# The start of a sorted-attention and maxout kernel on TensorE: queries loaded by head pair, the value turn inside the sinkhorn's waits, shared block-diagonal steps, weights in alternating quarters, fewer fillers, another order of the first item

## Chip, cores, metric

One core of a Trainium2 chip runs the whole kernel. The metric is device time in microseconds (us) of one execution; a kernel's number is the median of its runs. All intervals are 95%. Engines are called PE (TensorE), PEld (PE's weight loads), DVE (VectorE), ACT (ScalarE), POOL (GpSimd) and SP (SyncE), as in the profile.

## The reference

Four batch items of eight heads, 768 tokens and 64 features. A sinkhorn of five rounds turns each head's 8x8 matrix into P; keys and values are mixed block by block with P; each block of 96 queries attends to its own sorted block; the result goes through a maxout layer.

```python
for _ in range(5):                       # P: (B, H, 8, 8)
    P = exp(P - max(P, -1)); P /= sum(P, -1) + 1e-9; P /= sum(P, -2) + 1e-9
k_sorted = einsum('bhij,bhjcd->bhicd', P, k_blocks)      # same for v
attn = softmax(q_blocks @ k_sorted.T / 8) @ v_sorted     # inside each block
x = attn.transpose(0, 2, 1, 3).reshape(3072, 512)
out = maximum(x @ w1, x @ w2) @ w_out                    # float32 (3072, 512)
```

## The kernel before

The kernel computes max(x w1, x w2) w_out as relu(x (w1 - w2)) w_out + x (w2 w_out), so w1 is overwritten by the difference, a quarter at a time (`w_difference`), and w2 is transposed and multiplied with w_out once. All engines' lists are in program order. These are the parts that the argument touches. The first: matmuls on zeros ("fillers") whose only use is to keep PE busy, and the account by which evacuations of PSUM are dealt between ACT ("A") and DVE ("D").

```python
def keep_streaming(ps, n, by=None, most=512):      # n columns of zeros
    w0 = fill[:, 0:128] if by is None else late[by]
    while n > 0:
        w = min(n, most)
        nc.tensor.matmul(ps[:, 0:w], w0, fill[:, 0:w], start=True, stop=True)
        n -= w

load = {"A": 0.0, "D": 0.0}
def pick(a_ns, d_ns):
    if load["A"] + a_ns <= load["D"] + d_ns:
        load["A"] += a_ns; return "A"
    load["D"] += d_ns; return "D"
# ... evac(..., eng=None) asks pick() unless eng is given
def w_difference(t, eng=None):
    (eng or nc.vector).tensor_tensor(out=w1_sb[..quarter t..], in0=w1_sb[..],
                                     in1=w2_sb[..], op=ALU.subtract)
    if not eng:
        load["D"] += 600
```

The second: the beginning of the first batch item (cuts marked). `turn_v`, the "value turn", copies columns of the loaded values into the order in which the value sort reads them. The "products" or "hidden products" are the matmuls of x with the w1 difference; they go by chunks of half a batch item.

```python
keep_streaming(ps_f32("fill_ps"), 76 * 160, most=160)   # 76 matmuls of 160 columns
for it in range(5):
    sinkhorn(it)           # exp on ACT, six small steps on DVE; fillers from round 3 on
    if it == 0: masks(0)
    if it == 1: masks(1)
    if it == 2: selections(0); turn_v(first, "A", 0, 18)
    if it == 3: turn_v(first, "A", 18, 36)
turn_v(first, "A", 36, 56); turn_v(first, "A", 56, 80)
block_diagonals(0)         # P spread into the matrices that sort keys and values
turn_v(first, "D", 80, 96)
SC, VA, TR = att(0)        # scores, values, x transposes of item 0
sort_k(0, 0, 2048, "A"); sort_k(0, 1, 256, "D"); sort_k(0, 2, 256, "A")
# ... value sorts, query transposes, scores, values
moe_h_products(0, 0, 0, (0, 2), 256)
# ... x_transposes(0, 1), w_difference(1), products, w_difference(2),
# ... w2_transposes(0), w_difference(3), SC[5]
tail = {0: [VA[4]], 1: [SC[6], SC[7], VA[5]], 2: [VA[6], TR[2], VA[7]],
        3: [TR[3], w2_transposes(1), load_rest, block_diagonals(1)], ...}
```

The softmax here doesn't subtract the row's maximum and nothing guards it: scores larger than these inputs give would overflow.

## Time and profile before

| | before |
|---|---|
| median of the first 3 runs | 173.13 us (173.07 to 175.98) |
| profiled span, granted clock | 171.2 us, 1.00 |
| PE busy | 160.6 us, 94% |
| chain that ended last | PE 76%, DMA 14%, DVE 3% |

The share lines and the chain's pieces are shown and read in the prediction. Two more rows of the page of the kernel before matter; the second was passed over at the time. The first is the clock row: 40 equal slices of the span, the granted clock in tenths of full speed (9 is 90% or more). The second is from the list of DMA queues: queue and kind, packets, MB, share of 16 engines' span.

```profile
PEclk9999999999999999999999999999999999999999
...
q8 instruction: 15, 0.25, 0.6%
```

The clock was full in every slice. Queue q8 moved 15 transfers of 16 KB of the kind "instruction": parts of the program itself. That is 0.6% of the DMA engines' time, which looks like nothing.

### The profile page before, as it was taken

What the parts mean: (1) busy time and instruction counts of PE and PEld (TensorE: products, weight loads), DVE (VectorE), ACT (ScalarE), POOL (GpSimd) and SP (SyncE); (2) the same over time, 40 slices, a digit from 0 to 9 for tenths busy, and PEclk for the clock granted to TensorE, in tenths of its full rate; (3) what the DMA queues carried; (4) which work ended last, traced back from release to release, by engine and by line L of the source; (5) the groups of instructions that cost most, each with busy time, mean ns of one, the idle gap of its engine ahead of it and who ended that gap; (6) DMA issues with size and microseconds to landing.
All of it is one profiled execution on the core that took longest, in us unless ns stands there. A gap on an engine that the chain in (4) does not pass through costs nothing.

```text
span 171.2 us, 4489 instructions
## 1 busy us (share of the span) xinstructions
PE 160.6 (94%) x1984; PEld 97.5 (57%) x2002; DVE 83.8 (49%) x187; ACT 79.9 (47%) x96; POOL 22.9 (13%) x39
## 2 busy tenths in 40 slices
PE   7899698999999999999999999999999999999992
PEld 7847666665756555557565555566555545554452
DVE  5977796739552688401674636025653421340041
ACT  4577576786535353247875442245724224311100
POOL 7961352231402002000000000000000000000000
PEclk9999999999999999999999999999999999999999
DMA  3999999999999966999600261992022663000333
GB/s 47 201 205 205 201 209 204 216 203 206 223 209 205 203 98 170 127 221 289 75 4 0 50 169 67 151 256 54 0 38 70 150 176 121 8 0 0 123 123 123
DMA packets 29666, 23.09 MB, mean 135 GB/s; under 512 B 16656, under 2 KB 24592, under 8 KB 29648
## 3 DMA queue, kind: packets, MB, share of 16 engines
q0 software_dynamic: 10304, 12.58, 43.3%
q1 hardware_dynamic: 19200, 10.17, 24.7%
q8 instruction: 15, 0.25, 0.6%
q10 hardware_dynamic: 144, 0.07, 0.1%
q14 instruction: 3, 0.02, 0.1%
HBM read 25.17 MB, written 6.29 MB: 184 GB/s over the span
## 4 chain that ended last, share of the span: by engine, by line
PE 76%; DMA 14%; DVE 3%; ACT 2%; issue 2%; POOL 1%; DVEq 0%; ACTq 0%; POOLq 0%
PE out_ps L612 36%; PE h_ps L585 24%; DMA w_sb<-in_moe_w_dram 10%; PE wc_ps L563 4%; DMA v_raw<-in_v_dram 4%; PE o_ps L477 3%; PE s_ps L450 3%; PE k_ps L383 2%; ACT kT L104 1%; PE v_ps L404 1%; PE tq_ps L358 1%; PE v_ps L425 1%; ACT g L599 1%; DVE w_sb L191 1%; DVE kT L106 1%
## 5 line engine op out<-in xcount | busy, mean ns | idle before, releaser
L612 PE MATMUL out_ps<-wo_sb,g 128*128 128x512 bf16 (+2 forms) x188 | 46.1, 370 | 0.8 <-issue 0.3
L585 PE MATMUL h_ps<-xT,w_sb 128*128 128x384 bf16 x256 | 44.8, 326 | 1.4 <-ACT kT L104 0.5
L458 ACT ACTIVATE e<-s_ps 96x768 bf16<-96x768 f32 x32 | 24.2, 802 | 21.9 <-PE s_ps L450 21.7
L585 PEld LDWEIGHTS <-w_sb 128*128 128x128 bf16 x256 | 24.1, 98 | 17.2 <-issue 1.7
L612 PEld LDWEIGHTS <-g 128*128 128x128 bf16 x200 | 17.3, 98 | 16.5
L612 PE MATMUL out_ps<-wc,xT 128*128 128x512 bf16 (+2 forms) x99 | 24.7, 370 | 0.1
L601 DVE TENSOR_SCALAR g<-h_ps 128x768 bf16<-128x768 f32 x12 | 11.5, 958 | 25.0 <-PE h_ps L585 25.0
L599 ACT ACTIVATE g<-h_ps 128x768 bf16<-128x768 f32 x20 | 16.1, 812 | 15.0 <-PE h_ps L585 15.0
L104 ACT COPY o<-out_ps 128x1024 f32<-128x1024 f32 x10 | 10.1, 1012 | 27.1 <-PE out_ps L612 21.0
L494 DVE TENSOR_TENSOR x<-o_ps,rs 96x512 bf16<-96x512 f32 x32 | 22.0, 687 | 1.1
L612 PEld LDWEIGHTS <-xT 128*128 128x128 bf16 x100 | 9.6, 98 | 11.1
L488 DVE RECIPROCAL rs<-o_ps 96x8 f32<-96x8 f32 x32 | 6.4, 200 | 18.9 <-PE o_ps L477 18.9
L477 PEld LDWEIGHTS <-e 96*128 96x128 bf16 x256 | 11.4, 97 | 6.4 <-issue 1.0
L106 DVE CAST v_sb<-v_ps 96x1024 bf16<-96x1024 f32 x7 | 8.5, 1219 | 10.9 <-PE v_ps L425 9.8
L477 PE MATMUL o_ps<-v_sb,e 96*128 96x65 bf16 x256 | 12.6, 193 | 1.1 <-DVE w2T L106 0.7
L104 ACT CAST v_sb<-v_ps 96x1024 bf16<-96x1024 f32 x9 | 9.1, 1009 | 5.1 <-PE v_ps L404 5.0
L104 ACT CAST kT<-k_ps 128x1024 bf16<-128x1024 f32 x9 | 8.9, 1017 | 4.1 <-PE k_ps L383 4.1
L450 PE MATMUL s_ps<-qT,kT 64*128 64x96 bf16 x256 | 9.0, 204 | 1.0 <-DVE qT L106 1.0
L450 PEld LDWEIGHTS <-kT 64*128 64x128 bf16 x256 | 6.2, 94 | 5.6 <-issue 4.2
L82 PEld LDWEIGHTS <-fill 128*128 128x128 bf16 x84 | 7.2, 110 | 1.7 <-DVE fill L73 1.2
L82 PE MATMUL fill_ps<-fill 128*128 128x160 bf16 x76 | 6.7, 260 | 1.2 <-DVE fill L73 1.2
L145 POOL DMA_DIRECT2D k_raw<-in_k_dram x12 | 6.5, 544 | 8.1 <-DMA wo_sb<-in_moe_w_out_dram 3.9
(72 smaller groups left out, 127.7 us busy)
## 6 DMA issues: line engine op xcount, KB each, us to landing
out_dram<-o SPq DMA_DIRECT2D x11, 512.0 KB, 3.0
k_raw<-in_k_dram POOLq DMA_DIRECT2D x12, 256.0 KB, 12.4
q_raw<-in_q_dram POOLq DMA_DIRECT2D x4, 768.0 KB, 10.1
v_raw<-in_v_dram POOLq DMA_DIRECT2D x6, 384.0 KB, 12.7
w_sb<-in_moe_w_dram POOLq DMA_DIRECT2D x3, 512.0 KB, 15.6
wo_sb<-in_moe_w_out_dram POOLq DMA_DIRECT2D x2, 512.0 KB, 19.6
v_raw<-in_v_dram POOLq DMA_DIRECT2D x3, 256.0 KB, 5.0
w_sb<-in_moe_w_dram POOLq DMA_DIRECT2D x2, 256.0 KB, 13.9
```

The source lines that it names most:

```text
L82: nc.tensor.matmul(ps[:, 0:w], w0, fill[:, 0:w], start=True, stop=True)
L104: nc.scalar.copy(out=out_ap, in_=in_ap)
L106: nc.vector.tensor_copy(out=out_ap, in_=in_ap)
L450: nc.tensor.matmul(ps[:, h2 * 512 + ii * 128 : h2 * 512 + ii * 128 + BLK], kT[b][rows, (hp * 8 + i) * BLK : (hp * 8 + i) * BLK + 128], rhs ...
L458: nc.scalar.activation(out=e[:, 0 : 8 * BLK].rearrange("p (t c r) -> p t c r", t=8, r=R), in_=ps[0:BLK] .rearrange("p (t f) -> p t f", t=8 ...
L477: nc.tensor.matmul(ps[:, h2 * 512 + ii * 65 : h2 * 512 + (ii + 1) * 65], e[:, (h2 * 4 + ii) * BLK : (h2 * 4 + ii) * BLK + 128], v_sb[:, m0 ...
L494: nc.vector.tensor_tensor(out=x, in0=ov[:, :, :, 0:D], in1=rs.to_broadcast([BLK, 2, 4, D]), op=ALU.mult,)
L563: nc.tensor.matmul(wc_ps[0][:, m * 512 : (m + 1) * 512], w2T[:, fb, dmt * 128 : (dmt + 1) * 128], wo_sb[:, fb, :], start=(fb == 0), stop=( ...
L585: nc.tensor.matmul(h_ps[t][:, m * 512 : m * 512 + TCH], w1_sb[:, hp, fb * 128 : (fb + 1) * 128], xT[:, b % 2, ch, hp % 2, hp // 2, :], sta ...
L599: nc.scalar.activation(out=g, in_=src, func=AF.Relu)
L601: nc.vector.tensor_scalar(out=g, in0=src, scalar1=0.0, scalar2=None, op0=ALU.max)
L612: nc.tensor.matmul(dst, g_tiles[b, ch, m // 2][:, m % 2, off : off + 128] if m < NFB else xT[:, b % 2, ch, hp % 2, hp // 2, off : off + 12 ...
```

## The change

Its intent: have the queries of the first two head pairs sooner, take the value turn off ACT and put it where DVE waits for the sinkhorn's exponentials, spare DVE steps in the block-diagonal matrices, bring w1 and w2 in quarters in the order of use with the second subtraction on POOL, drop fillers that now seem superfluous, and order the first item's work accordingly. The core of the diff:

```diff
-    def load_q(b):
+    def load_q(b, by_pair=False):
...
+        for hs in [slice(hp, H, HP) for hp in range(HP)] if by_pair else [slice(0, H)]:
+            nc.gpsimd.dma_start(out=t[:, hs], in_=src[:, hs])
...
-    load_q(0)
-    load_w_columns(w2_sb, moe_w2, 0, 2)
-    load_w_columns(w1_sb, moe_w1, 0, 1)
-    load_w_columns(w1_sb, moe_w1, 1, 2)
+    load_q(0, True)
+    for t in range(2):
+        load_w_columns(w2_sb, moe_w2, t, t + 1)
+        load_w_columns(w1_sb, moe_w1, t, t + 1)
...
-    load_v(1)
...
     w_difference(0, nc.gpsimd)
+    w_difference(1, nc.gpsimd)
+    load_v(1)
...                                   # sinkhorn(it, meanwhile): called behind the exp
...                                   # block_diagonals: mult and reduce once for both kinds
-    keep_streaming(ps_f32("fill_ps"), 76 * 160, most=160)
+    keep_streaming(ps_f32("fill_ps"), 60 * 200, most=200)
+    c0 = 0
     for it in range(5):
-        sinkhorn(it)
-        if it == 0:
-            masks(0)
-        if it == 1:
-            masks(1)
+        if it < 2:
+            sinkhorn(it)
+            masks(it)
+            continue
+        sinkhorn(it, lambda: turn_v(first, "D", c0, c0 + 11))
+        c0 += 11
         if it == 2:
             selections(0)
-            turn_v(first, "A", 0, 18)
-        if it == 3:
-            turn_v(first, "A", 18, 36)
-    turn_v(first, "A", 36, 56)
-    turn_v(first, "A", 56, 80)
+        if it < 4:
+            turn_v(first, "A", c0, c0 + 18)
+            c0 += 18
+    turn_v(first, "A", c0, c0 + 19)
+    turn_v(first, "D", c0 + 19, BLK)
     block_diagonals(0)
-    turn_v(first, "D", 80, 96)
 
     SC, VA, TR = att(0)
-    sort_k(0, 0, 2048, "A")
-    sort_k(0, 1, 256, "D")
-    sort_k(0, 2, 256, "A")
+    sort_k(0, 0, 1536, "A")
+    sort_k(0, 1, 0, "D")
+    sort_k(0, 2, 0, "A")
...                                   # the rest of item 0 in another order:
     moe_h_products(0, 0, 0, (0, 2), 256)
+    SC[5]()
     x_transposes(0, 1, "A")
-    w_difference(1)
     moe_h_products(0, 0, 1, (0, 2))
+    moe_h(0, 0, 0, "A", (1, 3))
+    VA[4]()
+    moe_h(0, 0, 1, "A", (1, 3))
+    SC[6]()
+    VA[5]()
+    w_difference(2)
+    w2_transposes(0, "D")()
+    SC[7]()
+    w_difference(3)
+    VA[6]()
...
     tail = {
-        0: [VA[4]],
-        1: [SC[6], SC[7], VA[5]],
-        2: [VA[6], TR[2], VA[7]],
-        3: [TR[3], lambda: w2_transposes(1, "A")(), load_rest, lambda: block_diagonals(1)],
+        1: [TR[2], VA[7]],
+        2: [TR[3]],
+        3: [lambda: w2_transposes(1, "A")(), load_rest, lambda: block_diagonals(1)],
```

More of the change, by code (lines that the diff above doesn't have):

```diff
@@ L126 @@
         e_bufs.append(t)
-    def load_q(b):
+    def load_q(b, by_pair=False):
         t = qpool.tile([128, H, R * D], BF16, tag="q_raw", name="q_raw", bufs=1)
-        nc.gpsimd.dma_start(out=t, in_=q[b].rearrange("h (p r) d -> p h (r d)", r=R))
+        src = q[b].rearrange("h (p r) d -> p h (r d)", r=R)
+        for hs in [slice(hp, H, HP) for hp in range(HP)] if by_pair else [slice(0, H)]:
+            nc.gpsimd.dma_start(out=t[:, hs], in_=src[:, hs])
         q_raw[b] = t
@@ L224, with sinkhorn @@
     p_bf = const.tile([G, NB, NB], BF16, tag="p_bf", name="p_bf")
-    def sinkhorn(it):
+    def sinkhorn(it, meanwhile=None):
         nc.scalar.activation(out=p_sb, in_=p_sb, func=AF.Exp)
+        if meanwhile:
+            meanwhile()
         if it >= 3:
@@ L302, in block_diagonals @@
             )
-        for m in kinds:
-            pm = const.tile([128, NB, NB], FP32, tag=f"pm{m}", name="pm")
-            nc.vector.tensor_tensor(
-                out=pm,
-                in0=pe[:, m * 64 : m * 64 + 64].rearrange("p (i j) -> p i j", j=NB),
-                in1=maskJ[:, m].to_broadcast([128, NB, NB]).transpose([0, 2, 1]),
-                op=ALU.mult,
-            )
-            pt = const.tile([128, NB], FP32, tag=f"pt{m}", name="pt")
-            nc.vector.reduce_sum(out=pt, in_=pm, axis=AX.X)
+        n, m0 = len(kinds), min(kinds)
+        both = slice(m0, m0 + n)
+        pm = const.tile([128, n, NB, NB], FP32, tag=f"pm{n}", name="pm")
+        nc.vector.tensor_tensor(
+            out=pm,
+            in0=pe[:, m0 * 64 : (m0 + n) * 64].rearrange("p (m i j) -> p m i j", i=NB, j=NB),
+            in1=maskJ[:, both].to_broadcast([128, n, NB, NB]).transpose([0, 1, 3, 2]),
+            op=ALU.mult,
+        )
+        pt = const.tile([128, n, NB], FP32, tag=f"pt{n}", name="pt")
+        nc.vector.reduce_sum(out=pt, in_=pm, axis=AX.X)
+        for m in kinds:
             bd = const.tile([128, 8, NB], BF16, tag=f"bd{m}{b}", name="bd")
@@ L316, in block_diagonals @@
                 in0=maskM[:, m].to_broadcast([128, 8, NB]),
-                in1=pt.to_broadcast([128, NB, 8]).transpose([0, 2, 1]),
+                in1=pt[:, m - m0].to_broadcast([128, NB, 8]).transpose([0, 2, 1]),
                 op=ALU.mult,
@@ L685 @@
     sort_v(0, 2, 0, "A")
-    scores(0, 0)
+    SC[0]()
     sort_v(0, 3, 0, "D")
-    scores(0, 1)
+    SC[1]()
     q_transposes(0, 1, "D")
-    values(0, 0)
+    VA[0]()
     SC[2]()
@@ L693 @@
     SC[3]()
-    values(0, 2, 256)
+    VA[2]()
     x_transposes(0, 0, "A")
+    SC[4]()
     VA[3]()
-    SC[4]()
     moe_h_products(0, 0, 0, (0, 2), 256)
+    SC[5]()
     x_transposes(0, 1, "A")
-    w_difference(1)
     moe_h_products(0, 0, 1, (0, 2))
+    moe_h(0, 0, 0, "A", (1, 3))
[8 more added lines that the diff above has]
+    VA[6]()
     for b in range(1, B):
         selections(b)
-    w_difference(2)
-    w2_out = w2_transposes(0, "D")
-    moe_h(0, 0, 0, "A", (1, 3))
-    w2_out()
-    w_difference(3)
-    moe_h(0, 0, 1, "A", (1, 3))
-    SC[5]()
     def turn(rows, c0):
```

## The prediction

> **What bounds the kernel now.** I read the page of the kernel before first, for the engine shares, then the chain of waits in order of time, then the timelines of TensorE (PE), VectorE (DVE) and GpSimd (POOL) up to 40 us, then the landing time of each load. The page's first part:
>
> ```profile
> span 171.2 us, 4489 instructions
> PE 160.6 (94%) x1984; PEld 97.5 (57%) x2002; DVE 83.8 (49%) x187; ACT 79.9 (47%) x96; POOL 22.9 (13%) x39
> ```
>
> PE is idle for 171.2 - 160.6 = 10.6 us in all. The end behind the last matmul is about 3 us of that, and from 35 us on the chain is PE almost without a break. So only the first 35 us can give anything. The change edits just that stretch. Its chain of waits, columns start, length, what:
>
> ```profile
> 2.44 6.11 DMA v_raw<-in_v_dram
> ...
> 9.72 17.59 DMA w_sb<-in_moe_w_dram
> ...
> 27.40 0.69 DVE w_sb L191
> 28.09 1.13 DVE w2T L106
> 29.23 0.60 DVE w_sb L191
> ...
> 30.81 1.48 PE h_ps L585 x8
> ...
> 33.17 1.46 PE h_ps L585 x8
> 34.63 0.34 PE tx_ps L515 x8
> ```
>
> The reader is to see one DMA, the second half of w1, ending at 27.30, then three DVE steps behind it (subtract w2 from w1, evacuate the w2 transpose, subtract again), then PE. The timelines show where PE stops on the way (brackets: idle before, and what ended it):
>
> ```profile
> 16.28 0.86 PE L358 MATMUL tq_ps<-ident,q_raw 128*64 128x128 bf16 x24 [0.38 <-DMA q_raw<-in_q_dram]
> 18.20 0.35 PE L450 MATMUL s_ps<-qT,kT 64*128 64x96 bf16 x8 [0.48 <-DVE qT L106]
> ...
> 20.30 0.40 PE L477 MATMUL o_ps<-v_sb,e 96*128 96x65 bf16 x8 [0.35 <-DVE v_sb L106]
> 21.17 0.34 PE L450 MATMUL s_ps<-qT,kT 64*128 64x96 bf16 x8 [0.47 <-DVE qT L106]
> ...
> 29.28 0.40 PE L477 MATMUL o_ps<-v_sb,e 96*128 96x65 bf16 x8 [0.69 <-DVE w2T L106]
> ...
> 30.81 1.46 PE L585 MATMUL h_ps<-xT,w_sb 128*128 128x384 bf16 x8 [0.33 <-DVE rs L488]
> ```
>
> These gaps sum to 2.7 us. Filler matmuls between 12.5 and 24.3 us (1.04 us in front of the first key sort, then four of about 0.21) take 1.9 us that no result needs. That is the whole prize: at most 4.6 us, 2.7% of the time.
>
> **What the Trainium skill says.**
> (1) "TensorE: Matmul & The Clock Gate", Part 2: matmuls stay in program order, and Part 1 says the other engines' queues are strict first-in first-out. The trace agrees: every gap above is PE waiting for the next item of its list although later items were ready. So I can walk the new order by hand.
> (2) "SBUF — State Buffer", "Who interferes with whom": a DVE copy in a two-port mode and GpSimd (descriptor writing too) lock each other out. One copy agrees: sel_k took 0.53 us at 7.77, while a descriptor job ran, and 0.21 at 25.16. The value turn is safe by its rate: 512 words in 0.60 and 768 in 0.84 us is 0.94 ns a word[...].
> (3) "GPSIMD Engine Reference", section 3: an elementwise op of two inputs is about 2 times slower than on DVE. Here the same subtraction took 2.12 us on GpSimd and 0.68 on DVE, 3.1 times; I use the trace's.
> (4) The clock-gate page, Part 1: idling through a window of about 3.4 us halves the clock. Granted clock is 1.00 in all of my windows before; the longest new gap that I expect is 1.5 us, so it should stay.
>
> **The change part by part.**
>
> *Value turn on DVE.* Three times 11 columns, 11 x 32 = 352 words. From 0.60 - (160 x 0.00094) = 0.45 us each, about 0.40 from start to next start. The waits they are put in are partly filled already. In the third round the key masks end at 6.25 and the next reduce starts at 6.26: +0.39. In the fourth, the selections occupy it: about +0.3 to 0.4. In the fifth DVE idled 0.25 before 9.89: about +0.15. Sum: the normalisation ends some 0.85 us later, 12.2 in place of 11.33. ScalarE (ACT) is relieved, but it was done at 12.47 and values were first multiplied at 14.79, so that buys nothing.
>
> *Shared block-diagonal steps.* Multiply and reduce run once on 128 elements for two of 64. Rows: 0.23, 0.22 and 0.23 us for one kind; 64 more elements are [...]0.07 us. For keys that is 2 x 0.07 = +0.13; for values two steps of 0.26 go, less the 0.13. Two DVE steps fewer, but the key matrix, which PE awaits, comes later: 12.38 + 0.85 + 0.13, so key sorting starts near 13.45, not 12.50.
>
> *Fillers.* The first gives back at most 0.2 us (it ended at 12.57, the matrix was ready at 12.38); the two in front of the later key sorts 2 x 0.21. Key sorting then takes 3 x 0.62 and two value sorts 2 x 0.555: 2.97 us. Query transposes start at 13.45 + 2.97 = 16.4. Before: 16.28.
>
> *Queries by head pair.* The load of 768 KB was issued at 5.09 and landed at 16.24, 4.25 us after the last key piece (11.99). In quarters, the two pairs that the first transposes need should land near 14.1. That removes the 0.38 us wait, but with PE at 16.4 it no longer matters. Two more small parts of issue time (about 0.5 us each on POOL) stay hidden behind a DMA queue that is full (about 205 GB/s from 4 to 31 us).
>
> *Weights in alternating quarters.* Same bytes before the last of w1, so that lands again near 27.3. The first quarter of both comes after 512 in place of 768 KB: 1.3 us sooner (19 against 20.15). The first use, the product at 24.29, waited for the x transpose's evacuation (24.24), not for weights: hidden. The second subtraction on POOL runs 21.9 to 24.0 and saves DVE 0.6; its product comes at 25.5: hidden.
>
> *Order.* With S the start of the query transposes, everything up to the first product keeps the old offsets (scores at S + 1.9, products at S + 8.0), as the same evacuations bind. Then, with scores and products at 0.25 and 0.70 us, evacuations of 0.80 on ACT, and 0.87 for one normalisation on DVE: the sixth scores go in front of the second x transpose, so ACT does exp (to S + 9.8) before that transpose's copy (to 10.5); the rest of the first products waits for that, about 0.6 us of idle PE; values 4 and 5 reach DVE at S + 11.6 and 12.8. Only then comes the subtraction of quarter three, at S + 13.6 = 30.0, which started at 27.40 before. Behind it in DVE's list: w2T evacuation 1.15, subtraction 0.6, value 6 0.87, selections 0.6, value 7 0.87: to S + 18.3. The wait for the weights is gone, but DVE idled from S + 8.4 to 11.6, and the old wait (1.63 us) is of that kind too. PE has done its third hidden product by S + 16.4 and then meets the last x transpose, which needs value 7: a wait of 1.5 to 2 us. Before, this transpose stood behind the fourth hidden product and met no wait. Fourth product and last transpose are done at about S + 20.1 = 36.5; before at 34.80 (34.46 + 0.34).
>
> *Sum.* +1.7 us by the walk, to 174.8. I chose 174.0: the walk lets each hand-over cost a full latency and may overstate the last wait, and a tuner who ordered it so presumably had DVE ready sooner.
>
> **Rivals.**
> (a) The turn really fits in the waits and the early queries count. Then key sorting starts at 12.4, queries at 15.4, all is 1 us earlier, and DVE delays the end less: about 172. For it: the 0.38 us query wait and the 1.63 us weight wait are real. Against: DVE's rows have hardly any gap in rounds three and four.
> (b) PE's gaps all close and the fillers' time is used: 170 to 171. Against: four of six gaps are released by DVE, and the change takes from it only the subtraction (0.6), two small steps and no evacuation in this stretch.
> (c) More, smaller loads and a longer POOL list starve the queue, later loads come late: +1 to 2 us. Against: every lane has transfers outstanding; values and keys of batch 1 landed at 36.8 and 39.95 but are used at 39.0 and 43.5.
> (d) A PE pause in the normalisation drops the clock: +1 to 2 us. Against: point (4).
>
> **Range and chances.** Between (a) and the full walk with 1 us more: 171.9 to 175.9. Within 2% is 169.7 to 176.6. Faster needs 3.4 us of a prize of 4.6: 0.04. Slower needs twice the walk's loss: 0.06.
>
> **What would show it.** Sinkhorn's last multiply near 12.2 (right) or at 11.4 (turn free); first key-sort matmul near 13.45; query transposes near 16.4 with no wait for DMA; first subtraction on DVE near 30 with no DMA wait before it; an idle PE of over 1 us in front of the last batch-0 x transpose, released by DVE; products of the second chunk starting about 1 us later than 35.93. Wrong if DVE finishes value 7 well before PE reaches that transpose, or if the sinkhorn did not slip.

## The result and the profile after

| | before | after |
|---|---|---|
| median | 173.10 us (172.85 to 175.98, 4 runs) | 181.67 us (179.73 to 181.84, 4 runs) |
| ratio | | 1.0456 [1.0372, 1.054] |
| span, clock of the profiled run | 171.2 us, 1.00 | 180.0 us, 0.96 |

A ratio is the mean time of one kernel's runs over that of the other's runs of the same rounds, so it isn't quite the ratio of the medians. Executions over 1.5% slower than the fastest of the same kernel are left out of the means. The change makes the kernel 8.6 us slower; the prediction had 0.9 us.

The page of the changed kernel: share lines, clock row, and the shares of the chain that ended last.

```profile
span 180.0 us, 4454 instructions
...
PE 165.8 (92%) x1964; PEld 100.4 (56%) x1982; DVE 83.9 (47%) x185; ACT 79.2 (44%) x95; POOL 28.3 (16%) x44
...
PEclk9999555899999999999999999999999999999999
...
PE 80%; DVE 11%; issue 4%; ACT 3%; DMA 1%; DVEq 0%; ACTq 0%
```

PE has 20 fewer matmuls than before and is busy 5.2 us longer: the clock row says why, three slices (18 to 31.5 us) at half speed. DMA has left the chain (14% before, 1% now), so the wait for the weights did go; DVE and "issue" stand there instead. "Issue" is time in which an engine waited for nothing that the profile shows. PE's timeline shows where it lies (start, length, line, operation, out<-in, count; in brackets the idle time before and what ended it):

```profile
13.15 1.71 PE L388 MATMUL k_ps<-bd,k_raw 64*64 64x64 bf16 x96 [0.21 <-DVE bd L319]
...
15.83 0.69 PE L363 MATMUL tq_ps<-ident,q_raw 128*64 128x128 bf16 x17
19.32 0.59 PE L363 MATMUL tq_ps<-ident,q_raw 128*64 128x128 bf16 x7 [2.81 <-issue]
...
40.52 0.51 PE L520 MATMUL tx_ps<-ident,x 96*128 96x96 bf16 x8 [1.35 <-DVE x L499]
```

PE does 17 of 24 equal query transposes, stands for 2.81 us in the middle of them with data and PSUM at hand, and goes on. The last line is the wait that the prediction expected, with its 1.35 us. The table by stretches of the changed kernel, then of the one before (stretch, its length, busy time and count of PE, PEld, DVE, ACT and POOL, granted clock, DMA share, GB/s):

```profile
14.00:18.00 4.00, 2.52 (x104) 2.27 (x97) 2.35 (x2) 2.92 (x3) 2.22 (x3) 1.00 1.40 197
18.00:20.00 2.00, 0.68 (x11) 0.51 (x11) 0.05 (x1) 0.00 (x0) 0.47 (x1) 0.72 1.47 196
20.00:33.00 13.00, 12.38 (x164) 9.10 (x163) 6.54 (x11) 7.19 (x9) 7.88 (x9) 0.52 1.24 210
```

```profile
18.00:20.00 2.00, 1.75 (x56) 1.61 (x56) 1.11 (x2) 2.00 (x3) 0.53 (x1) 1.00 1.45 201
20.00:33.00 13.00, 10.95 (x178) 7.98 (x178) 10.03 (x24) 8.38 (x12) 5.14 (x6) 1.00 1.23 210
```

In the 13 us behind the stop PE is busy 12.38 us for 164 matmuls, before 10.95 us for 178, at clock 0.52 in place of 1.00. The transfers carry the same 210 GB/s in both, so the DMA queues for data are not starved.

What did PE stand for? All its data had been there: the four pieces of the queries landed at 12.88, 13.86, 14.93 and 15.86 us, and PE stopped at 16.51. PE had by then started 448 instructions (matmuls and weight loads counted together, as the trace records them). Counting the "instruction" transfers beside it gives the lead. The DMA view (queue, packets, MB, share), first of the kernel before from 13.3 to 14.3 us, then of the changed one from 12.5 to 16.9 and from 16.9 to 18.0:

```profile
q0 software_dynamic: 244, 0.19, 123.8%
q8 instruction: 1, 0.02, 5.9%
```

```profile
q0 software_dynamic: 1421, 0.86, 136.2%
q14 instruction: 1, 0.01, 0.5%
```

```profile
q0 software_dynamic: 412, 0.20, 137.7%
q8 instruction: 1, 0.02, 5.4%
```

Before, the first 16 KB transfer of q8 runs from 13.35 to 14.29 us, and PE starts its 448th instruction at 15.65. After, there is none of q8 until 17.03; it runs to 17.98, and PE resumes at 19.32. The kernels have some 3,950 to 4,050 PE instructions and 15 or 16 such transfers, so one carries about 256 instructions of 64 bytes.

The Trainium skill, "Runtime: NRT & Kernel Launch", section "Instruction fetch mechanics", says that an engine's sequencer refills its instruction memory in 16 KiB blocks of 256 instructions over a DMA queue of its own, the next block while the current one executes, and that the cost is "mostly hidden". The sizes agree with this trace; "hidden" does not.

### The profile page after: what moved, and what is told of

Read it like the earlier page. It is cut to its first block, busy times and chain, and to the rows that moved or that the text cites. A ratio compares the mean times of both kernels' runs of the same rounds, so it can differ in the third digit from the quotient of the medians.

```text
span 180.0 us, 4454 instructions
## 1 busy us (share of the span) xinstructions
PE 165.8 (92%) x1964; PEld 100.4 (56%) x1982; DVE 83.9 (47%) x185; ACT 79.2 (44%) x95; POOL 28.3 (16%) x44
## 4 chain that ended last, share of the span: by engine, by line
PE 80%; DVE 11%; issue 4%; ACT 3%; DMA 1%; DVEq 0%; ACTq 0%
PE out_ps L617 34%; PE h_ps L590 24%; PE s_ps L455 4%; PE o_ps L482 4%; PE wc_ps L568 4%; PE k_ps L388 2%; ACT kT L104 2%; PE v_ps L409 2%; PE tq_ps L363 2%; DVE x L499 1%; PE tx_ps L520 1%; DVE qT L106 1%; PE v_ps L430 1%; DMA p_sb<-in_sort_net_dram 1%; PE fill_ps L82 1%
## 5 line engine op out<-in xcount | busy, mean ns | idle before, releaser
L590 PE MATMUL h_ps<-xT,w_sb 128*128 128x384 bf16 x256 | 46.0, 332 | 1.2 <-ACT kT L104 0.5
L604 ACT ACTIVATE g<-h_ps 128x768 bf16<-128x768 f32 x22 | 17.8, 811 | 18.3 <-PE h_ps L590 18.2
L606 DVE TENSOR_SCALAR g<-h_ps 128x768 bf16<-128x768 f32 x10 | 9.6, 958 | 26.0 <-PE h_ps L590 26.0
L106 DVE CAST v_sb<-v_ps 96x1024 bf16<-96x1024 f32 x9 | 10.9, 1217 | 6.3 <-PE v_ps L409 5.0
L106 DVE CAST kT<-k_ps 128x1024 bf16<-128x1024 f32 x5 | 6.0, 1223 | 12.6 <-PE k_ps L388 12.6
L455 PE MATMUL s_ps<-qT,kT 64*128 64x96 bf16 x256 | 10.4, 217 | 1.1 <-DVE qT L106 0.5
L104 ACT CAST v_sb<-v_ps 96x1024 bf16<-96x1024 f32 x7 | 7.1, 1010 | 4.6 <-PE v_ps L409 4.0
L132 POOL DMA_DIRECT2D q_raw<-in_q_dram x7 | 5.8, 838 | 20.7 <-DVE q_pair L341 13.3
L104 ACT CAST kT<-k_ps 128x1024 bf16<-128x1024 f32 x7 | 6.9, 1015 | 4.3 <-PE k_ps L388 4.3
L82 PE MATMUL fill_ps<-fill 128*128 128x200 bf16 x60 | 7.3, 299 | 1.2 <-DVE fill L73 1.2
```

The lines of the kernel that those rows point to most:

```text
L104: nc.scalar.copy(out=out_ap, in_=in_ap)
L106: nc.vector.tensor_copy(out=out_ap, in_=in_ap)
L455: nc.tensor.matmul(ps[:, h2 * 512 + ii * 128 : h2 * 512 + ii * 128 + BLK], kT[b][rows, (hp * 8 + i) * BLK : (hp * 8 + i) * BLK + 128], rhs ...
L590: nc.tensor.matmul(h_ps[t][:, m * 512 : m * 512 + TCH], w1_sb[:, hp, fb * 128 : (fb + 1) * 128], xT[:, b % 2, ch, hp % 2, hp // 2, :], sta ...
L604: nc.scalar.activation(out=g, in_=src, func=AF.Relu)
L606: nc.vector.tensor_scalar(out=g, in0=src, scalar1=0.0, scalar2=None, op0=ALU.max)
```

## The experiments

**The theory.** The changed kernel runs out of program. It has 32 fewer PE instructions at the very start (60 fillers of 200 columns in place of 76 of 160; each filler is a matmul and a weight load). The request for the next block is made when PE reaches a fixed place in its list, here somewhere near its 160th to 190th instruction (an inference, narrowed down under a_quiet: no record shows the request). In the changed kernel this place lies behind the wait for the key matrix at 13.15 us; PE then runs through the key sort, the value sorts and 17 transposes in 3.4 us without one wait, and the block is late. The pause in turn halves the clock. The prediction's own mechanism, a later DVE chain and order, is the remaining part.

**The rivals.** (R1) The load of queries in four pieces stops PE in a way that the profile doesn't name. (R2) Order and turn cost nearly all of the 8.6 us, and clock and stop are side shows. (R3) The clock falls by chance, independently of the stop.

The first four kernels ran on one chip, with the kernel before at 173.38 us (7 runs).

### a_100fills: the change with more and shorter fillers

```diff
-    keep_streaming(ps_f32("fill_ps"), 60 * 200, most=200)
+    keep_streaming(ps_f32("fill_ps"), 100 * 120, most=120)
```

The columns, and so the filling time, stay at 12,000; the instructions rise by 80.

> The changed kernel with its first filler run cut into 100 matmuls of 120 columns in place of 60 of 200 (same 12000 columns), so that PE's list is 80 instructions longer before the stop. Theory 'program piece' (PE stops at its 449th instruction because the next 16 KB of its program come late, asked for 256 instructions before): the ask now falls inside the fillers near 7.5 us, so no stop of over 0.5 us in the query transposes, granted clock 1.00, and a time of 174 to 176 (the walk of the prediction). Rival 'data' (the second query pair or some semaphore really came late): the stop stays near 16.5 us, about 2.8 us long, and the time stays near 181.

Measured: 175.78 us (175.74 to 175.82), ratio 1.0128 [1.0091, 1.0165], clock 1.00 in every run. PE's timeline of this kernel:

```profile
15.92 0.86 PE L363 MATMUL tq_ps<-ident,q_raw 128*64 128x128 bf16 x24
...
34.49 0.51 PE L520 MATMUL tx_ps<-ident,x 96*128 96x96 bf16 x8 [1.35 <-DVE x L499]
```

All 24 transposes run without a break, as the theory forecast; the first program block came from 10.44 to 11.38 us; 5.9 of the 8.6 us are gone. The wait of 1.35 us remains. R2 falls: order and turn can account for at most the 2.4 us that are left.

### a_76fills: the change with the old fillers

```diff
-    keep_streaming(ps_f32("fill_ps"), 60 * 200, most=200)
+    keep_streaming(ps_f32("fill_ps"), 76 * 160, most=160)
```

> The changed kernel with the old first filler run (76 matmuls of 160), which is 32 instructions more. Theory 'program piece': PE stops again after exactly 448 instructions, which is now about the second query transpose in place of the 17th, for 2 to 3.5 us; clock under 1, time 178 to 183. Rival 'data': it stops at the same 17th transpose as before, or not at all.

Measured: 177.51 us (176.68 to 179.42; the last one slow), ratio 1.0264 [1.0186, 1.0343]. PE's timeline:

```profile
15.88 0.24 PE L363 MATMUL tq_ps<-ident,q_raw 128*64 128x128 bf16 x1
16.74 0.83 PE L363 MATMUL tq_ps<-ident,q_raw 128*64 128x128 bf16 x23 [0.61 <-issue]
```

The stop moved from the 17th transpose to behind the first: 16 fillers more, 16 transposes earlier. It stays at the same count of instructions, about 450, and not at the same operation. It is shorter (0.61 us), because the block came from 14.27 to 15.22 us. Here the forecast missed in size: it had a stop of 2 to 3.5 us, a clock under 1 and 178 to 183 us, and the profiled run has clock 1.00. The old fillers alone do not protect the new kernel; a likely reason, not tested alone, is that it has also dropped fillers from the key sort and with them time in which the block could come.

### b_60fills: the kernel before with the change's fillers

```diff
-    keep_streaming(ps_f32("fill_ps"), 76 * 160, most=160)
+    keep_streaming(ps_f32("fill_ps"), 60 * 200, most=200)
```

> The kernel before with only the new first filler run (60 matmuls of 200), 32 instructions fewer. Theory 'program piece, by place alone': PE stops about 32 instructions later in the list, at the 17th query transpose, for 1 to 3 us, time 176 to 181. If the split loads are needed as well to make the piece late: no stop and 173.

Measured: 177.80 us (177.12 to 177.94), ratio 1.0236 [1.0194, 1.0279], clock 0.96. PE's timeline:

```profile
16.06 0.58 PE L358 MATMUL tq_ps<-ident,q_raw 128*64 128x128 bf16 x14
18.45 0.74 PE L358 MATMUL tq_ps<-ident,q_raw 128*64 128x128 bf16 x10 [1.81 <-issue]
```

One line of fillers, with nothing else of the change, costs 4.4 us. The stop comes behind the 14th transpose, not the 17th as forecast, but again at 448 instructions (this kernel has two more fillers in its key sort and one in front of it), and a block ran from 16.19 to 17.14 us. The clock was at 0.50 in 18 to 20 us and at 0.56 on average in 20 to 33: R3 falls too, since the stop brings this long low clock into a kernel that had none. Why so little tips it: in the kernel before, PE started its 448th instruction 1.36 us after the block's transfer had ended, and in the four profiles with a stop (the changed kernel, a_76fills, a_q_whole and this one) it resumed 1.31 to 1.52 us after that end. The tuned kernel had next to no slack to lose.

### a_q_whole: the change with one load of the queries

```diff
-    load_q(0, True)
+    load_q(0)
```

> The changed kernel with the queries in one load again. If the small loads crowd the piece of program out: the piece's transfer starts before 15 us, the stop goes, about 175. If the place in the list alone decides: the stop of 2 to 3 us after 448 instructions stays, time 179 to 182.

Measured: 181.39 us (181.19 to 181.54), ratio 1.045 [1.0411, 1.049], clock 0.96. PE's timeline:

```profile
19.31 0.59 PE L363 MATMUL tq_ps<-ident,q_raw 128*64 128x128 bf16 x7 [2.68 <-issue]
```

The same stop, at the same place. R1 falls. Loading by head pair neither causes the loss nor gains anything that can be seen (181.67 with it), since the queries were not what PE waited for.

The next four ran on a second chip, with the kernel before at 173.12 us (7 runs).

### a_quiet: the change with the DMA queues empty when the block is asked for

```diff
+        if by_pair:
+            nc.scalar.copy(out=t[:, 0, 0:1], in_=kT[0][:, 0:1])
...
     sort_k(0, 2, 0, "A")
+    load_q(0, True)          # all loads of queries and weights issued only here,
+    ...                      # behind the first sorted keys
```

> The changed kernel with the loads of queries and weights held back until the first sorted keys are copied, so that the DMA engines are idle from about 12 to 15 us. Slower on purpose. If data traffic is what delays the 16 KB piece: its transfer starts within 1 us of the start of the key sort (13.2 to 14.5 us), not near 17.0. If the ask itself comes late whatever the traffic: near 17.

Not meant to be fast (the queries come late by design): 184.21 us. The DMA view from 14.0 to 15.3 us has the block as the only transfer:

```profile
q8 instruction: 1, 0.02, 5.2%
```

With 0 GB/s from 12 to 14 us it started at 14.12, in place of 17.03; PE had reached its place in the list at 13.16 to 13.41 in both (160th and 192nd instruction: 13.16 and 13.41 here, 13.16 and 13.43 in the changed kernel). So from there to the start it is 0.7 to 1.0 us on idle queues and 3.6 to 3.9 us beside 198 GB/s of data. The other traces narrow the place down: counted from PE's 166th instruction, the first block starts 2.9 to 3.8 us later in all thirteen other profiles, and 0.9 us later here; counted from the 190th, it would be 0.85 us in the kernel before and 3.6 in the changed one, both beside traffic. The second blocks agree: they start 3.0 to 3.8 us after PE's 448th instruction, or after the resumption where PE stopped there, in all fourteen (3.7 in the kernel before; 3.3 in this one, by then beside 173 GB/s). What holds it up in the DMA engines isn't shown.

### a100_tr3: a_100fills with the last x transpose later

```diff
     tail = {
         1: [TR[2], VA[7]],
-        2: [TR[3]],
-        3: [lambda: w2_transposes(1, "A")(), load_rest, lambda: block_diagonals(1)],
+        3: [TR[3], lambda: w2_transposes(1, "A")(), load_rest, lambda: block_diagonals(1)],
```

> The 100-filler form of the changed kernel with the last x transpose of batch 0 behind the fourth hidden product again, as in the kernel before. The prediction's walk: the 1.35 us that PE waits there for DVE is filled with the product, 1.0 to 1.4 us faster than the 100-filler form (175.8), so 174.4 to 174.8. Rival (DVE's lateness just moves to the next wait): within 0.3 us of 175.8. No stop with 'issue' as its cause is expected.

Measured: 174.62 us (174.42 to 175.28), ratio 1.0093 [1.0038, 1.0148]. PE's timeline:

```profile
34.40 0.51 PE L520 MATMUL tx_ps<-ident,x 96*128 96x96 bf16 x8
```

The wait of 1.35 us is gone, and the median is 1.2 us below that of a_100fills (another chip and round; the intervals of the ratios overlap). The traces agree: the second-chunk products start at 35.87 us in place of 37.26. The prediction's last step, a PE that meets the transpose before DVE has done value 7, is real and worth 1.2 to 1.4 us here.

### a100_turnA: a_100fills with the value turn as it was

```diff
+        sinkhorn(it)
         if it < 2:
-            sinkhorn(it)
             masks(it)
...
+            turn_v(first, "A", 0, 18)          # and so on, as in the kernel before
```

> The 100-filler form with the value turn as in the kernel before (on ScalarE, and 16 columns on DVE behind the block diagonals). Walk: the sinkhorn no longer slips, ends near 11.3 instead of 11.8, all later work 0.5 to 0.9 us earlier: 174.9 to 175.3. Rival (the slip is hidden by a later wait): within 0.3 us of 175.8.

Measured: 175.42 us (174.84 to 175.68), ratio 1.0122 [1.0075, 1.0169]. The sinkhorn's last multiply starts at 10.99 us in place of 11.72 (a_100fills), and the key sort at 12.43 in place of 13.25. Nearly all of it is lost again, and the median lies between the two forecasts. In the profiled run the clock fell to 0.72 in 20 to 26 us, although PE had no pause over 0.5 us in the stretch before (1.18 us busy of 18 to 20); and the 1.35 us wait came back unchanged:

```profile
34.70 0.51 PE L520 MATMUL tx_ps<-ident,x 96*128 96x96 bf16 x8 [1.35 <-DVE x L499]
```

That transpose ran at 34.70, against 34.49 with the new turn. A miss for the simple view that DVE's 0.7 us at the start comes out at the end. The two runs at full clock took 174.84 and 175.33 us, so the turn is worth 0.4 to 0.9 us at most.

### d_best: the useful parts together

The old turn, 88 fillers of 136 columns, value 4 and scores 5 ahead of the second pair of products, and the last x transpose later (against a_100fills; scores 6 and 7 and values 5 and 6 move too, and the 256 filler columns of the first products go).

```diff
-    keep_streaming(ps_f32("fill_ps"), 100 * 120, most=120)
+    keep_streaming(ps_f32("fill_ps"), 88 * 136, most=136)
...
     x_transposes(0, 1, "A")
+    VA[4]()
+    SC[5]()
     moe_h_products(0, 0, 1, (0, 2))
...
+        3: [TR[3], lambda: w2_transposes(1, "A")(), load_rest, lambda: block_diagonals(1)],
```

> A version meant to beat both: split query loads, weight quarters and shared block-diagonal steps of the change; value turn as before; 88 fillers of 136 columns; the fifth values in front of the sixth scores, so that DVE has work while ScalarE copies; last x transpose behind the fourth product. Walk: query transposes start near 15.4, fourth product and last transpose are done near 33.5 in place of 34.8: 171.5 to 173.0. If the program piece is late again (PE stops after 448 or 704 instructions): 174 or more.

Measured: 174.45 us (173.81 to 175.68), ratio 1.0079 [1.002, 1.0138]: not better than before, and outside the 171.5 to 173.0 forecast. The stretches of it:

```profile
20.00:26.00 6.00, 5.61 (x84) 4.05 (x85) 3.66 (x11) 3.71 (x5) 5.52 (x6) 0.72 1.26 207
```

There was no stop for program, and the clock fell all the same, to 0.50 from 22.30 us for 3.41 us. PE is short of work between the first scores and values (1.25 us busy of 18 to 20; 1.75 in the kernel before). That this is the reason is likely from d_best2 below. Whether the old order's fillers at 22.08 and 23.86 us would have prevented it, no run shows.

The next three ran on a third chip, with the kernel before at 173.46 us (11 runs, one slow).

### a100_load: a_100fills with the evacuations dealt as before

```diff
     w_difference(1, nc.gpsimd)
+    load["D"] += 600
```

> The 100-filler form with one line of bookkeeping: the 600 ns that the second weight subtraction no longer takes from DVE are counted on DVE again, so that every later PSUM evacuation goes to the same engine as in the kernel before. Theory (of its 2.4 us over the kernel before, some 1.5 are lost by 36 us and the other 1.0 later, because the evacuations were dealt out differently): 174.6 to 175.0, 0.8 to 1.2 us under 175.8. Rival (the rest is lost elsewhere): 175.5 to 176.

`w_difference` on POOL adds nothing to DVE's account, so from there on the dealing takes DVE for 600 ns freer than it was, and every later choice can shift. With the line, the choices are the same as in the kernel before, evacuation by evacuation (compared in the two traces). Measured: 175.03 us (174.79 to 175.87), ratio 1.0095 [1.0056, 1.0134]. The chain of waits at the sorted keys of item 1 (start, length, what), first of a_100fills, then of this kernel:

```profile
45.53 1.94 ACT kT L104 x2
```

```profile
46.27 1.24 DVE kT L106
```

In a_100fills two key evacuations of 0.97 us follow each other on ACT, and PE waits 0.29 us for the second; dealt as before, ACT and DVE alternate. It is one place of several. Behind the kernel before, a_100fills lags by 1.33 us at the second-chunk products and by 2.46 at the first products of the last batch item (142 us); this kernel by 1.56 and 1.74. So the dealing costs some 0.95 us in the traces. By the medians it is 175.78 - 175.03 = 0.75 us; the two ran in different rounds and the intervals of their ratios overlap, so the size is likely rather than proven.

### d_best2: d_best with that line and with fillers in PE's gaps

```diff
+    load["D"] += 600
...
-    SC[0]()
+    scores(0, 0, 512)
...
-    VA[0]()
-    SC[2]()
+    values(0, 0, 512)
+    scores(0, 2, 512)
...
-    VA[2]()
+    values(0, 2, 512)
...
-    moe_h_products(0, 0, 0, (0, 2))
+    moe_h_products(0, 0, 0, (0, 2), 256)
```

> The version meant to beat both (d_best) with the same bookkeeping line, and with fillers put back in the waits between 17 and 24 us (four of 512 columns, one of 256), because the granted clock fell to 0.79 there in d_best. If clock and evacuations were what ate its gain: clock 1.00 and 171.3 to 172.6. If the fillers only delay: 173 or more.

Measured: 171.88 us (171.72 to 172.41), ratio 0.9906 [0.9872, 0.9941]. The stretches of it:

```profile
20.00:26.00 6.00, 5.42 (x90) 3.52 (x89) 4.28 (x10) 4.51 (x6) 5.95 (x6) 1.00 1.26 206
```

With five fillers, 2,304 columns that no result needs, PE is busy 1.74 us of 18 to 20, and the clock stays at 1.00 where d_best had 0.72 (at least 0.997 in all six runs, 0.978 to 0.99 in the four of d_best). The accounting line came in with them, and no run parts the two. This version beats both kernels, by 0.9% (clear of the noise, if small) and by some 5%. Its second-chunk products start at 34.41 us (before: 35.93), so the change's loads and shared steps, with the old turn and yet another order, can go with a gain of about 1.5 us. Part of that comes without the change: the next run, of the same round, is at 172.54 with nothing but more fillers at the start.

### b_100fills: the control

```diff
-    keep_streaming(ps_f32("fill_ps"), 76 * 160, most=160)
+    keep_streaming(ps_f32("fill_ps"), 100 * 120, most=120)
```

> Control: the kernel before with its first filler run as 100 matmuls of 120 columns. Its program pieces are then asked for earlier than in the kernel before. If cutting the fillers has no effect of its own: within 0.5 us of 173.2, no stop with 'issue' in the transposes.

Measured: 172.54 us (172.31 to 174.01), ratio 0.9948 [0.9905, 0.999]. More and shorter fillers do no harm in the old order, and a_100fills' distance from before is not theirs. It is 0.66 us under the 173.2 of the forecast, a little outside the band of 0.5, and the interval of the ratio lies just under 1: the fillers even help somewhat. Like with like, 100 fillers in both and the same round, a100_load is 175.03 - 172.54 = 2.5 us behind this kernel. Four of six runs had clock 1.00; two had 0.99 and took 173.69 and 174.01, so a run with a little less clock costs some 1.2 to 1.6 us (against the 172.44 us that the other four average), with no stop for program in the profiled one. Its trace shows what 0.99 is: one stretch of 3.41 us at clock 0.50 (from 18.85 us). a100_turnA, d_best and the profiled run of a100_busy have one such stretch each; the changed kernel, a_q_whole and b_60fills have one of 13.65 us, four times as long.

The last ran on the first chip again, with the kernel before at 173.85 us (12 runs).

### a100_busy: the same delay with PE busy

To part the stop from the clock, a_100fills got 13 fillers of 512 columns at the point of the stop.

```diff
     sort_v(0, 1, 0, "A")
+    keep_streaming(ps_f32("fill_ps"), 6656)
     q_transposes(0, 0, "D")
```

> The 100-filler form (175.8, no stop) with 13 filler matmuls of 512 columns, 13 x 0.213 = 2.8 us, in front of the first query transposes: the same delay at the same place as the stop of the changed kernel, but with PE busy, so the clock should stay at 1.00. Theory (of the 5.9 us between the changed kernel and its 100-filler form, 2.8 are the stop itself and the other 3.1 the halved clock that follows): 178.2 to 179.0 at clock 1.00. Rival (the delay itself costs more than its length, the clock nothing): 181 to 182.

Measured: 178.77 us (178.74 to 179.87), ratio 1.0304 [1.0269, 1.0339]; four runs had clock 1.00 and took 178.74 to 178.79. The profiled run is one of the other two (0.99), but its low stretch begins only at 25.49 us. PE's timeline:

```profile
15.87 2.98 PE L82 MATMUL fill_ps<-fill 128*128 128x512 bf16 x12
18.78 0.86 PE L363 MATMUL tq_ps<-ident,q_raw 128*64 128x128 bf16 x24
```

The fillers (12 of the 13 are in the record) take 2.98 us and the transposes start at 18.78 in place of 15.92, 2.86 us later. At full clock this costs 178.75 - 175.78 = 2.97 us: nothing of it is made up later. So of the 5.9 us between the changed kernel and a_100fills, the idle stop of 2.81 us is about 2.8, and the 3.1 that are left are the halved clock. One run of the changed kernel checks this: it had clock 0.99, so one low stretch of 3.41 us in place of four (an estimate: half of 3.41 us is 1% of its 178), and took 179.73 us; 179.73 - 175.78 - 2.81 leaves 1.1 us for that one.

## Why the prediction was wrong

The 181.67 - 173.10 = 8.57 us divide like this, each from the runs above:

| part | us | from |
|---|---|---|
| stop for the program block | 2.8 | its length; a100_busy shows that such a delay comes out in full |
| clock halved after it | 3.1 | changed kernel less a_100fills, 5.9, less the stop |
| order, turn, loads and shared steps, with 100 fillers | 1.6 | a100_load less before, same round |
| evacuations dealt otherwise | 0.75 | a_100fills less a100_load |
| rest | 0.35 | the medians of the kernel before in these two rounds, 173.46 less 173.10 |

The third row contains what 100 fillers gain by themselves: against b_100fills it would be 2.5 us. Its parts were not all tested alone.

By the prediction's own steps:

- **Sinkhorn slip and key matrix.** Right in kind, too large. It had 0.85 us; the last multiply starts at 11.61 in place of 11.12, a slip of 0.49. The timeline of DVE in the changed kernel shows the value turn in the fifth round and the last multiply:

```profile
9.99 0.45 DVE L213 COPY v_dc<-v_raw 64x352 uint32<-64x352 uint32 x1
...
11.61 0.21 DVE L241 TENSOR_TENSOR p_bf<-p_sb,colsum 32x64 bf16<-32x64 f32 x1
```

  The three copies took 0.44 to 0.45 us as predicted, each beside a descriptor job of POOL and not slowed, but more of them lay in real waits. (A fourth piece, 0.37 us at 11.76, was not in the walk.) The shared multiply and sum took 0.29 us each, 0.06 to 0.07 more than for one kind, as predicted. Key sorting began at 13.15 (predicted 13.45), the query transposes at 15.83 (16.4), with no wait for a DMA, as it said.
- **The walk to the second chunk.** Right in its steps. Without the stop (a_100fills) the subtraction on DVE is at 29.81 (predicted 30.0) with no DMA in front of it, PE waits 1.35 us for value 7 (1.5 to 2), and the second-chunk products start at 37.26, 1.3 us later than before (about 1). The walk's +1.7 us stands beside a measured 1.6, or 2.5 like with like (b_100fills), so the close agreement is in part luck.
- **The step that failed: fillers and clock.** The part *Fillers* counted what the fillers give back in time, 0.2 us and 2 x 0.21, and took them for nothing else. They are also instructions, and their number sets where PE stands in its program when the work without waits begins. Point (4), "the longest new gap that I expect is 1.5 us, so it should stay", rested on a list of data waits; a gap of 2.81 us with no data wait in it was in none of the steps, nor the 3.1 us that the halved clock cost behind it. Even the walk itself held a longer gap than 1.5 us, the wait of 1.5 to 2 for value 7. So rival (d), a pause that drops the clock for 1 to 2 us, was set aside by point (4). It was the nearest to the truth, in the wrong place (the pause was in the query transposes, not the normalisation) and with 5.9 us for stop and clock together.
- **Readings that were off.** None of these decided the outcome. Five of the six gaps shown are released by DVE, not four. The filler of 1.04 us ran from 11.53 to 12.57, and by the walk itself only 0.2 of it could come back, so the prize was nearer 3.7 us than 4.6. Splitting the query load adds three issues on POOL, not two (3.11 us in place of 0.92). Key sort and two value sorts took 2.68 us, not 2.97. And the pair of sel_k copies doesn't show a lock between DVE and GpSimd: the fast one, at 25.16, also began beside a descriptor job (24.74 to 25.27).
- **What was not looked at.** The removed entry in the load account, worth some 0.75 to 0.95 us, could be read from the diff: the 600 ns are added only if no engine is named.
- **The shading.** The choice of 174.0 below the walk's 174.8 rested on a guess about the tuner; a100_load (175.03, with before at 173.46) gives no support for it.

What remains open: what delays a 16 KB block by about 3 us beside data traffic; what exactly the sequencer's request is tied to; and what sets off the single low stretch of 3.41 us in some runs of several versions, the kernel before included (clock 0.99).

## What to carry to other kernels

Fillers and other cheap PE work are program as well as time: when you remove or merge them just ahead of a long stretch without waits, count PE's instructions up to there, look for the "instruction" rows of the DMA queues and for idle time with the releaser "issue", and leave the block some 6 us from the point where PE can ask for it (an estimate: 3.7 us to its start, 0.95 for its transfer and 1.3 to the resumption, all as measured here beside 200 GB/s). A gap of 1.8 to 2.8 us cost two to two and a half times its length here (4.4 us for 1.81, 5.9 for 2.81), since the clock drops behind it; fillers in the gaps were cheap against that (d_best2). And when work moves to another engine, keep the account by which later work is dealt, or each later choice moves with it.

## What the Trainium skill lacked or had wrong

- "Runtime: NRT & Kernel Launch", section "Instruction fetch mechanics", calls the cost of crossing a block boundary "mostly hidden". Here PE stood 2.81, 2.68, 1.81 and 0.61 us at a boundary, each time at about the 448th of its instructions. The page gives PE room for 2,048 instructions, and in a note below it speaks of only two lines of 16 KiB; a PE that stops at its 448th has not been supplied 2,048 ahead. It lacks that the block is late beside data: it started 0.9 us after PE's 166th instruction on idle queues, 2.9 to 3.8 us beside some 200 GB/s, and PE resumed 1.31 to 1.52 us after its end.
- "TensorE: Matmul & The Clock Gate", Part 1, gives about 3.4 us of idling for the clock to halve, and its last section advises against gaps over about 3 us. Here stops of 1.81 us (b_60fills, 0.50 in 18 to 20 us) and 2.81 us (0.52 over the next 13 us) were enough; in b_60fills the clock fell 1.15 us into the stop. With gaps of at most 0.5 us but PE busy only 1.18 us of 2 (a100_turnA) the clock also fell, to 0.72 in the next 6 us. Part 1 does mention that frequent micro-idling makes the clock oscillate; it gives no share of busy time for it.
- "GPSIMD Engine Reference", section 3, puts an elementwise step with two inputs at about 2 times DVE's time. Here the same subtraction took 3.1 times (2.12 us on POOL, 0.68 on DVE, 128x1024 in bf16; the page's factor is measured in float32).
- No page says how to see a program stop in a profile. Here it is idle PE time with the releaser "issue" between two equal instructions, with a 16 KB transfer of an "instruction" queue ending 1.3 to 1.5 us before PE resumes.
